# A two-stage spectral mix and a gated FFN on one core: unstrided PSUM columns and a hand-ordered opening

## Chip, cores, metric

One core of one Trainium2 chip runs the whole program. The metric is the device time of one execution in microseconds (us), as a median over runs. Engines are named as in the profile: PE is TensorE's matmuls, PEld its weight loads, DVE is VectorE, ACT is ScalarE, POOL is GpSimd, SP is the engine whose queue issues most DMAs; "SPq" is its queue.

## The reference

```python
X = np.fft.fft(x, axis=1)            # x: 8 batches x 3008 positions x 256 channels, fp32
X = np.fft.fft(X, axis=2).real       # keep the real part
x = X.reshape(24064, 256)
g, val = x @ w_gate, x @ w_val       # 256 -> 1536 each
out = (0.5 * g * (1 + erf(g / sqrt(2))) * val) @ w_out      # exact GELU, 1536 -> 256
```

## The kernel before

The transforms are done as matmuls with bf16 tables (G, CS, TPI) that the kernel computes itself with sines at its start. 3008 = 94 x 32 = 64 x 47, so one batch passes through these stages, each a small "pack" of matmuls into one PSUM tile followed by an evacuation:

- stage one, 16 packs: x (94 rows) against G, 96 columns a matmul, into A;
- second stage (CH), 12 packs: A against CS, 256 columns a matmul, into Z;
- E and O packs, 3 and 6: Z against TPI, 64 columns (E) or 2 x 64 columns (O), for 24 values k2, into EO. EO holds the even and odd halves of the tokens, in 23 x 64 + 33 columns.

The FFN then works on EO in three chunks of 512, 512 and 481 columns. Its first layer makes a result from E and O together, hands it to GELU and the product, and then adds a third matmul (weights M) on top of the same PSUM to get the mirrored tokens. The second layer sums 12 matmuls of 256 columns into the output. While batch b is in the FFN, the packs of batch b+1 are put between its matmuls as filler, so PE always has something to do.

The columns of neighbouring k2 are interleaved, so that a pair of them can be stored with one DMA whose rows are 2 KB:

```python
# cols: (offset in PSUM, k2, step, width) -- two k2 share 128 columns, alternating
if i + 1 < len(gr) and width(gr[i]) == width(gr[i + 1]):
    col += [(o, gr[i], 2, K1), (o + 1, gr[i + 1], 2, K1)]
...
def e_pack(gi):
    ps = ps_dft()
    for off, k2, step, n in cols[gi]:
        nc.tensor.matmul(_sub(ps, [[step, n]], off), Z[:, k2, 0:128], TPI[:, 0:n], ...)
    nc.scalar.activation(EO[E columns], ps[:, :n], AF.Copy)          # ScalarE evacuates E
def o_pack(gi, half):
    ps = ps_dft()
    for off, k2, step, n in part:
        nc.tensor.matmul(_sub(ps, [[256, 2], [step, n]], off - base), Z[:, k2, 128:256], TPI..., ...)
    nc.vector.tensor_copy(EO[O columns], ps[:, 256:256 + n])         # VectorE evacuates O
```

The opening. The first half of batch 0's x comes plain (fp32, SP's queue) and is cast by VectorE; the second half comes through GpSimd's queue, which casts on the way:

```python
load_x_plain([(0, 4), (4, 4), (8, 8)])            # SP: j 0..15, fp32
load_x(0, [(NJS, 8), (NJS + 8, 8)])               # GpSimd: j 16..31, cast by the DMA
...
gen_g(0, 8); cast_x(0, 4); gen_g(8, 24); cast_x(4, 4); cast_x(8, 8)
...                                               # w_gate, w_val by SP, w_out by GpSimd
for w in head[:NS1]: w()                          # stage one of batch 0
gen_cs(); gen_t()
for w in head[NS1:NHEAD]: w()                     # five CH packs, E and O of the first chunk
for nm in ("g", "v"): fold_w(nm, 0)()             # weights W: fold by an fp32 matmul, 512 columns
...
for b in range(B):
    if b + 1 < B:
        x_tiles.append(x_tile()); load_x(b + 1, [(0, 16), (16, 16)])   # GpSimd, casting
```

## Time and profile before

| | before |
|---|---|
| device time, median of 3 | 773.95 us (773.54 to 774.24) |
| span of the profiled run | 771.8 us |
| first first-layer matmul | 31.18 us |
| time from one batch's first first-layer matmul to the next, batches 2 to 6 | 91.5 us |

The page's busy table, and its chain of work that ended last:

```profile
PE 745.8 (97%) x5324; PEld 491.1 (64%) x5324; DVE 488.4 (63%) x829; ACT 442.1 (57%) x829; POOL 18.1 (2%) x39
...
PE 93%; ACT 2%; DMA 1%; DVE 1%; issue 1%; SPq 0%; ACTq 0%; DVEq 0%
```

PE is busy for 97% of the span and is 93% of the chain. So two things are worth working on: PE's own occupancy, and an earlier begin of the steady stage.

The groups by shape of the E (L376) and O (L389) matmuls. Columns: line, engine, operation, tiles, shape and count, then busy us and mean ns of one:

```profile
L350 PE MATMUL ps_dft<-CS,A_sb 128*128 128x256 bf16 x384 | 60.5, 280 | 0.3 <-ACT A_sb L332 0.3
...
L389 PE MATMUL ps_dft<-TPI,Z_sb 128*128 128x128 bf16 x184 | 26.7, 302 | 0.2 <-ACT EO_sb L379 0.2
...
L376 PE MATMUL ps_dft<-TPI,Z_sb 128*128 128x64 bf16 x184 | 16.9, 241 | 0.3 <-DVE Z_sb L360 0.3
```

The mean of an O matmul of 128 columns (302 ns) is longer than that of a contiguous CH matmul of 256 columns (280 ns). The records of neighbouring matmuls overlap (O matmuls start 109 ns apart, with records of 302 ns in the mean), so the better reading is from start to start.

The chain of waits through the opening, followed back from 34 us (start us, length us, what):

```profile
3.35 11.28 DMA wg_hi<-in_moe_w_gate_dram
...
14.76 2.05 PE ps_g L300 x2
...
17.45 1.71 PE ps_v L300 x2
...
24.30 4.80 PE ps_dft L350 x20
```

Two fp32 folds (PE ps_g and ps_v, L300) stand between stage-one packs (in the program's text they follow the CH packs; the trace shows the order that ran), and the five CH packs take 4.80 us: 20 matmuls, most of them 213 ns apart where the steady stage has 109. The clock records of this trace have TensorE at half rate there: half rate from 22.31 to 29.14 us, then full rate. Below, a stage is called cold when its CH matmuls stand 213 ns apart, warm when they stand 109 ns apart. The steady stage begins here:

```profile
31.18 0.42 PE L449 MATMUL ps_g<-EO_sb,WgE 128*128 128x512 bf16 x1
```

### The profile page before, as it was taken

The numbers are of one execution on the slowest core, as the hardware profiler recorded it, in microseconds if no ns is written. First come the engines' busy times: TensorE is split into PE (matmuls) and PEld (weight loads), VectorE is DVE, ScalarE is ACT, GpSimd is POOL, SyncE is SP. The second block draws the span as 40 slices with busy tenths as digits, with TensorE's granted clock in tenths as the row PEclk, the third lists the DMA queues.
The fourth block names the chain that finished last, engine by engine and source line by source line (L and its number), as shares of the span: only waits on it lengthen the run. The fifth ranks groups of instructions, "written<-read, shape, count | busy, mean of one in ns | idle before, by whom it ended". The sixth has DMA issues, their size and how long they took to land.

```text
span 771.8 us, 13825 instructions
## 1 busy us (share of the span) xinstructions
PE 745.8 (97%) x5324; PEld 491.1 (64%) x5324; DVE 488.4 (63%) x829; ACT 442.1 (57%) x829; POOL 18.1 (2%) x39
## 2 busy tenths in 40 slices
PE   3899999999999999999999999999999999999996
PEld 1555676666666666666666666666666666666565
DVE  6588666665666665766666666666566666655550
ACT  5656555555655555555655555555555555655552
POOL 6000000000000000000000000000000000000000
PEclk9899999999999999999999999999999999999999
DMA  9900501050101510114101320101010111011111
GB/s 237 237 12 24 112 28 42 28 118 28 43 28 39 112 38 28 42 38 108 41 30 42 78 69 28 42 28 40 28 42 29 39 36 34 28 42 38 42 42 65
DMA packets 32756, 42.54 MB, mean 55 GB/s; under 512 B 3770, under 2 KB 29370, under 8 KB 31282
## 3 DMA queue, kind: packets, MB, share of 16 engines
q1 hardware_dynamic: 29332, 29.34, 11.3%
q0 software_dynamic: 3360, 12.34, 8.4%
q8 instruction: 41, 0.67, 0.4%
q14 instruction: 23, 0.19, 0.1%
HBM read 29.36 MB, written 24.64 MB: 70 GB/s over the span
## 4 chain that ended last, share of the span: by engine, by line
PE 93%; ACT 2%; DMA 1%; DVE 1%; issue 1%; SPq 0%; ACTq 0%; DVEq 0%
PE ps_o L485 32%; PE ps_v L449 9%; PE ps_g L449 8%; PE ps_g L465 8%; PE ps_v L465 8%; PE ps_v L450 8%; PE ps_g L450 8%; PE ps_dft L350 5%; PE ps_dft L321 3%; PE ps_dft L389 3%; DMA wg_hi<-in_moe_w_gate_dram 1%; PE ps_dft L376 1%; ACT gelu_sb L469 1%; ACT gelu_sb L452 1%; DVE h_sb L453 1%
## 5 line engine op out<-in xcount | busy, mean ns | idle before, releaser
L453 DVE TENSOR_TENSOR h_sb<-gelu_sb,ps_v 128x512 bf16<-128x512 bf16 (+1 forms) x288 | 195.1, 678 | 203.7 <-ACT gelu_sb L452 138.3
L485 PE MATMUL ps_o<-Wo_sb,h_sb 128*128 128x256 bf16 (+1 forms) x2304 | 298.4, 273 | 0.0
L485 PEld LDWEIGHTS <-h_sb 128*128 128x128 bf16 (+1 forms) x2304 | 227.7, 100 | 74.4 <-issue 2.7
L452 ACT ACTIVATE gelu_sb<-ps_g 128x512 bf16<-128x512 f32 (+1 forms) x288 | 169.4, 588 | 161.8 <-PE ps_g L450 160.4
L471 DVE TENSOR_TENSOR h_sb<-gelu_sb,ps_v 128x512 bf16<-128x512 bf16 (+1 forms) x288 | 193.5, 672 | 45.0 <-ACT gelu_sb L469 42.6
L469 ACT ACTIVATE gelu_sb<-ps_g 128x512 bf16<-128x512 f32 (+1 forms) x288 | 169.2, 588 | 46.9 <-PE ps_g L465 44.9
L465 PE MATMUL ps_g<-EO_sb,WgM 128*128 128x512 bf16 (+1 forms) x288 | 110.0, 382 | 1.2 <-ACT gelu_sb L452 0.7
L449 PE MATMUL ps_g<-EO_sb,WgE 128*128 128x512 bf16 (+1 forms) x288 | 107.9, 375 | 1.3
L465 PE MATMUL ps_v<-EO_sb,WvM 128*128 128x512 bf16 (+1 forms) x288 | 108.2, 376 | 0.6
L449 PE MATMUL ps_v<-EO_sb,WvE 128*128 128x512 bf16 (+1 forms) x288 | 107.8, 374 | 0.8
L450 PE MATMUL ps_g<-EO_sb,WgO 128*128 128x512 bf16 (+1 forms) x288 | 108.1, 375 | 0.0
L450 PE MATMUL ps_v<-EO_sb,WvO 128*128 128x512 bf16 (+1 forms) x288 | 108.0, 375 | 0.0
L494 ACT ACTIVATE out_sb<-ps_o 128x512 f32<-128x512 f32 x96 | 57.3, 597 | 85.0 <-PE ps_o L485 85.0
L321 PEld LDWEIGHTS <-x_sb 94*128 94x128 bf16 x512 | 36.5, 100 | 44.4 <-issue 11.4
L350 PE MATMUL ps_dft<-CS,A_sb 128*128 128x256 bf16 x384 | 60.5, 280 | 0.3 <-ACT A_sb L332 0.3
L321 PE MATMUL ps_dft<-G,x_sb 94*128 94x96 bf16 x512 | 45.1, 210 | 13.8 <-ACT G L230 10.1
L350 PEld LDWEIGHTS <-A_sb 128*128 128x128 bf16 x384 | 37.8, 100 | 26.1 <-DVE A_sb L334 2.0
L360 DVE CAST Z_sb<-ps_dft 128x512 bf16<-128x512 f32 x69 | 47.2, 685 | 6.1 <-PE ps_dft L350 6.1
L334 DVE CAST A_sb<-ps_dft 128x384 bf16<-128x384 f32 x90 | 49.5, 552 | 1.8 <-PE ps_dft L321 1.5
L450 PEld LDWEIGHTS <-WvO 128*128 128x128 bf16 x288 | 28.0, 97 | 32.1 <-issue 11.1
L449 PEld LDWEIGHTS <-WvE 128*128 128x128 bf16 x288 | 28.2, 98 | 25.8 <-issue 1.1
L450 PEld LDWEIGHTS <-WgO 128*128 128x128 bf16 x288 | 28.1, 98 | 17.7 <-issue 8.4
(72 smaller groups left out, 318.1 us busy)
## 6 DMA issues: line engine op xcount, KB each, us to landing
out_dram<-out_sb SPq DMA_DIRECT2D x176, 128.0 KB, 2.0
x_sb<-in_x_dram POOLq DMA_DIRECT2D x14, 752.0 KB, 10.2
out_dram<-out_sb SPq DMA_DIRECT2D x16, 64.0 KB, 2.0
wg_hi<-in_moe_w_gate_dram SPq DMA_DIRECT2D x3, 256.0 KB, 9.1
wv_hi<-in_moe_w_val_dram SPq DMA_DIRECT2D x3, 256.0 KB
wg_lo<-in_moe_w_gate_dram SPq DMA_DIRECT2D x3, 256.0 KB, 8.5
wv_lo<-in_moe_w_val_dram SPq DMA_DIRECT2D x3, 256.0 KB
Wo_sb<-in_moe_w_out_dram POOLq DMA_DIRECT2D x2, 384.0 KB, 12.9
```

The lines of the kernel that those rows point to most:

```text
L321: nc.tensor.matmul(ps[:, jj * 96 : (jj + 1) * 96], xt[:, j0 + jj, cc * 128 : (cc + 1) * 128], G[:, j0 + jj, :], start=True, stop=True,)
L334: nc.vector.tensor_copy(dst, src)
L350: nc.tensor.matmul(ps[:, d * C : (d + 1) * C], A[:, cc, k2 + d, :], CS[:, cc, :], start=(cc == 0), stop=(cc == 1),)
L449: nc.tensor.matmul(ps[:, :n], W[nm, "E"][:, fs], EO[:, 0, c0 : c0 + n], start=True, stop=False)
L450: nc.tensor.matmul(ps[:, :n], W[nm, "O"][:, fs], EO[:, 1, c0 : c0 + n], start=False, stop=True)
L452: nc.scalar.activation(gl[:, :n], pg[:, :n], AF.Gelu)
L453: nc.vector.tensor_tensor(st["h"][:, fc, 0, :n], gl[:, :n], pv[:, :n], op=ALU.mult)
L465: nc.tensor.matmul(ps[:, :n], W[nm, "M"][:, fs], EO[:, 1, c0 : c0 + n], start=False, stop=True, skip_group_check=True)
L469: nc.scalar.activation(gl[:, :n], pg[:, :n], AF.Gelu)
L471: nc.vector.tensor_tensor(_sub(st["h"], [[-1, n]], (fc * 2 + 1) * TOK + n - 1), gl[:, :n], pv[:, :n], op=ALU.mult)
L485: nc.tensor.matmul(pso[:m, sign, :], st["h"][:, fc, sign, h0 : h0 + m], Wo_sb[:, fc, :], start=(fc == 0), stop=(fc == NFC - 1),)
L494: nc.scalar.activation(osb[:m], pso[:m], AF.Copy)
```

## The change

Its intent is to have PE write PSUM columns side by side, and to end the opening earlier. The whole of the first x is loaded plain by 96 rows (two of them only pad the count) and cast on VectorE and ScalarE; every engine's order in the opening is written by hand; the tables are computed with fewer, longer, contiguous calls; stage one and the five CH packs rotate over eight PSUM buffers instead of two; the first fold is 128 columns and the second 384. The stores double in number, since two k2 are no longer neighbours.

```diff
-            if i + 1 < len(gr) and width(gr[i]) == width(gr[i + 1]):
-                col += [(o, gr[i], 2, K1), (o + 1, gr[i + 1], 2, K1)]
-                ...
+        for k2 in gr:
+            col.append((o, k2, width(k2)))
+            o += width(k2)
@@ E pack, O pack
-                        _sub(ps, [[step, n]], off), ...
+                        ps[:, off : off + n], ...
-                        _sub(ps, [[256, 2], [step, n]], off - base), ...
+                        _sub(ps, [[256, 2], [1, n]], off - base), ...
@@ store: one DMA for each k2
-                ap=[[N2 * C, hi - lo], [1, n2 * C]],
+                ap=[[N2 * C, hi - lo], [1, C]],
@@ first x
-    xs = work_pool.tile([NP, NJS, C], ...)            # half of x, 94 rows in pieces of 80 and 14
+    xs = [work_pool.tile([96, NJ // 2, C], ...) for _ in range(2)]    # all of x
@@ PSUM of the opening
+    def ps_any(b):        # batch 0, first 24 packs: rotate over the tags dft, g, v, o
@@ opening
+    with tc.manual_schedule():
+        load_x_plain([(0, 4), (4, 4), (8, 8), (16, 8), (24, 8)])
+        load_w(); gen_consts()
+        g_phase(0, 8); g_sin(0, 8); cast_x(0, 4); g_phase(8, 24); s1_run(0)
+        cast_x(4, 4); cs_phase(); g_sin(8, 24); s1_run(4); cast_x(8, 8)
+        t_phase(); cs_sin(); t_sin()          # t_sin also loads GELU's table
+        ...                                   # keep, keep2
+        s1_run(8); s1_run(12)
+        cast_x(16, 4); cast_x(20, 4, True); s1_run(16)        # True: on ScalarE
+        cast_x(24, 4); cast_x(28, 4, True); s1_run(20); s1_run(24); s1_run(28)
+        for w in head[NS1:NHEAD]: w()
+        for nm in ("g", "v"): fold_w(nm, 0)()
+        ...
+        load_wo()
... (the table code itself, the column constants and the slots of the folds are cut)
```

Nothing in the diff touches the load of batch 1's x, but nothing holds it back either: GpSimd's queue used to be busy with half of batch 0's x and with w_out, and is now free.

## The prediction

> **What bounds the kernel now.** TensorE: the busy table has PE at 97% of a 771.8 us span, DVE 63%, ACT 57%, and the chain that ended last is 93% PE. From about 31 us (first first-layer matmul, L449, at 31.18 in the timeline) to 765 us the PE runs nearly back to back; in the windows 45-740 us it is busy 98-100%. So there are two places to win: shorter PE occupancy in the steady stage, and an earlier end of the opening.
>
> **PSUM columns unstrided (the larger part).** The E matmuls (L376, 64 columns) and O matmuls (L389, 2x64 columns) write PSUM at step 2. Read start to start in the trace, a 128-column O matmul holds the PE for 109 ns, just like the contiguous 256-column second-stage matmul L350 (109 ns), and a 64-column E matmul for 56 ns; the contiguous 33-column E and 66-column O ones take 30 ns. So strided writing runs at half speed. [...] Unstrided I estimate 56 and 29 ns: 53 + 27 = 80 ns per k2. 23 k2 x 7 batches x 80 ns = 12.9 us in the steady stage, and about 1.2 us for what batch 0 does after the opening. Those packs are filler between first-layer matmuls on a saturated PE, so nearly all of it counts; I deduct 1.5 us for slots that will then wait for GELU or an evacuation. The output stores double in number (each half as large, same 1 KB packets), off the chain.
>
> **Opening.** Now: DVE idles until 4.66 us, because the x cast stands first in its queue; the cosine table then needs ACT calls of 0.7-0.8 us for 192 elements and 1.55 us for 576 (strided bf16 writes), so the first matmul starts at 10.07; x pieces land at 4.6, 9.5, 14.2 us; two fp32 folds (2.05 and 1.91 us) sit between stage-one packs; stage one ends at 24.3; the second stage then runs at a clock of 0.59 (windows 25-30). After: tables first and half as many, contiguous ACT calls, first matmul near 5.5 us; stage one uses eight PSUM buffers, folds come later and the first is 128 columns wide, GELU's table load (1.28 us at 32.91) is early. But the order of instructions shows batch 1's x load (casting queue) right after the constants, near 3-4 us, without a wait: it shares the DMA engines with x, so I expect the last x piece at 17-20 us, stage one ending near 20-21, and a cold second stage again. First L1 matmul near 27 us: gain 4 us. The 384-column folds may give about 1 us back in the first slots.
>
> **Sum.** 773.95 - 12.9 - 1.2 + 1.5 - 4 + 1 = 758 us. Range 751 to 766. Chances: faster by over 2% 0.5, within 2% 0.48, slower 0.02.
>
> **What would show it.** O matmuls 56 ns apart and E near 30 (mean durations 302 to about 222, 241 to about 195 ns); steady windows shorter by 1.8 us per batch; first L1 matmul at 25-29 us; stage-one evacuations unchanged at 552 (DVE) and 492 ns (ACT).
>
> **What would make it wrong.** Stage-one evacuations now read PSUM one element at a time (step 48 between neighbours): if that is slower, DVE fills and PE waits (stage-one slots already hold most PE stalls). Weight loads, not columns, may bound E matmuls. The x load contention may eat the opening's gain, or prove mild and double it; Wo is now loaded last and could stall the second layer.

The sum: its 80 ns for each k2 is the estimate from the distances that stand before it, and the sum is 758 us (758.35 unrounded).

## More of the kernel before

The timeline of before around the first E and O packs in batch 1 (start us, length us, engine and line; only PE, DVE and ACT are copied):

```profile
177.25 0.61 PE L376 MATMUL ps_dft<-TPI,Z_sb 128*128 128x64 bf16 x8
...
177.66 0.41 PE L465 MATMUL ps_g<-EO_sb,WgM 128*128 128x512 bf16 x1
...
177.89 0.60 ACT L379 ACTIVATE EO_sb<-ps_dft 128x512 bf16<-128x512 f32 x1 [0.23 <-PE ps_dft L376]
177.91 0.38 PE L465 MATMUL ps_v<-EO_sb,WvM 128*128 128x512 bf16 x1
...
178.12 0.60 PE L389 MATMUL ps_dft<-TPI,Z_sb 128*128 128x128 bf16 x4
178.39 0.59 ACT L469 ACTIVATE gelu_sb<-ps_g 128x512 bf16<-128x512 f32 x1
...
178.52 0.42 PE L465 MATMUL ps_g<-EO_sb,WgM 128*128 128x512 bf16 x1
...
178.78 0.38 PE L465 MATMUL ps_v<-EO_sb,WvM 128*128 128x512 bf16 x1
...
179.03 0.38 PE L449 MATMUL ps_g<-EO_sb,WgE 128*128 128x512 bf16 x1
```

Eight E matmuls hold PE from 177.25 to 177.66: 0.41 us. Four O matmuls hold it from 178.12 to 178.52: 0.40 us, 109 ns each after the first. The 512-column matmul behind each pack then holds PE for longer than its usual 0.216 us: 0.25 us (177.66 to 177.91) and 0.26 us (178.52 to 178.78).

## The result, and the profile after

| | before | after |
|---|---|---|
| device time, median | 773.75 us (773.54 to 774.24) | 765.73 us (765.58 to 766.20) |
| ratio after : before | | 0.9897 [0.9879, 0.9914] |
| span of the profiled run | 771.8 us | 763.8 us |
| first first-layer matmul (weights WgE) | 31.18 us | 32.04 us |
| from there to the end | 740.6 us | 731.8 us |
| batch to batch, batches 2 to 6 | 91.5 us | 90.3 us |

The gain is 8 us, half of what was forecast. It lies 0.3 us inside the slow end of the range, and that is partly luck: the range was wide enough to take in an opening that lost time instead of gaining 4 us. A ratio is the mean time of one kernel's fast runs over that of the other's of the same rounds, so it is not quite the ratio of the medians quoted; brackets hold its 95% interval.

The busy table and the chain of after:

```profile
PE 733.6 (96%) x5328; PEld 477.1 (62%) x5328; DVE 490.1 (64%) x834; ACT 442.6 (58%) x828; POOL 12.4 (2%) x30
...
PE 91%; ACT 3%; DMA 3%; DVE 2%; issue 1%; SPq 0%; ACTq 0%
```

PE has lost 12.2 us of busy time and its share of the chain has gone down, while ACT, DMA and DVE have gained shares. That is the first sign that part of what PE gave up has come back as waiting.

The same groups by shape after:

```profile
L385 PE MATMUL ps_dft<-TPI,Z_sb 128*128 128x128 bf16 x184 | 17.3, 219 | 0.5 <-ACT EO_sb L375 0.5
...
L372 PE MATMUL ps_dft<-TPI,Z_sb 128*128 128x64 bf16 x184 | 12.1, 193 | 0.2
```

302 ns became 219 and 241 became 193, as forecast (about 222 and 195). The timeline at the same place of batch 1:

```profile
176.69 0.40 PE L372 MATMUL ps_dft<-TPI,Z_sb 128*128 128x64 bf16 x8
...
176.92 0.38 PE L457 MATMUL ps_g<-EO_sb,WgM 128*128 128x512 bf16 x1
...
177.12 0.60 ACT L375 ACTIVATE EO_sb<-ps_dft 128x512 bf16<-128x512 f32 x1
177.14 0.38 PE L457 MATMUL ps_v<-EO_sb,WvM 128*128 128x512 bf16 x1
...
177.14 0.69 DVE L445 TENSOR_TENSOR h_sb<-gelu_sb,ps_v 128x512 bf16<-128x512 bf16 x1 [1.33 <-ACT gelu_sb L444]
177.35 0.39 PE L385 MATMUL ps_dft<-TPI,Z_sb 128*128 128x128 bf16 x4
...
177.58 0.38 PE L457 MATMUL ps_g<-EO_sb,WgM 128*128 128x512 bf16 x1
...
177.61 0.59 ACT L461 ACTIVATE gelu_sb<-ps_g 128x512 bf16<-128x512 f32 x1
...
177.88 0.38 PE L457 MATMUL ps_v<-EO_sb,WvM 128*128 128x512 bf16 x1
...
178.26 0.38 PE L441 MATMUL ps_g<-EO_sb,WgE 128*128 128x512 bf16 x1
```

The E pack holds PE for 0.23 us (176.69 to 176.92) and the O pack for 0.23 us (177.35 to 177.58), each about half of before, and the matmul behind the E pack is back at 0.22 us. But the next two matmuls wait. The one at 177.88 adds to ps_v, which the product on DVE (177.14 to 177.83) is still reading; the one at 178.26 takes the ps_g that GELU on ACT (177.61 to 178.20) is still reading, and that GELU stood behind E's evacuation (L375, from 177.12). From the start of the E pack to the matmul at 178.26 it is 1.57 us; the same piece of before (177.25 to 179.03) took 1.78 us. Two packs and their tails that became 0.42 us cheaper (0.41 + 0.03 to 0.23, and 0.40 + 0.04 to 0.23) gained 0.21 us here.

The chain through the opening of after:

```profile
2.58 19.72 DMA x_plain<-in_x_dram
...
22.33 0.70 DVE x_sb L225
...
23.93 0.88 ACT A_sb L329 x2
...
24.86 1.20 PE ps_g L347 x4
```

The first first-layer matmul of after:

```profile
32.04 0.39 PE L441 MATMUL ps_g<-EO_sb,WgE 128*128 128x512 bf16 x1
```

One DMA of x is on the chain for 19.72 us, until 22.31 us. What SP's queue waits for in the first 40 us shows the same (total us, times, longest us), before and then after:

```profile
SPq L285 <- DMA x_plain<-in_x_dram: 6.4, 3, 3.8
```

```profile
SPq L268 <- DMA x_plain<-in_x_dram: 16.1, 4, 6.2
```

The last piece of x landed at 22.3 us (before: 13.9). From 8 to 22 us the packets of batch 1's x, in GpSimd's queue, are in the trace beside those of batch 0's. SP's queue moves 524 to 574 KB in 2 us while it is alone and 213 to 311 KB while both are busy, about half.

### The profile page after: what moved, and what is told of

Read it like the earlier page. It is cut to its first block, busy times and chain, and to the rows that moved or that the text cites. A ratio compares the mean times of both kernels' runs of the same rounds, so it can differ in the third digit from the quotient of the medians.

```text
span 763.8 us, 14086 instructions
## 1 busy us (share of the span) xinstructions
PE 733.6 (96%) x5328; PEld 477.1 (62%) x5328; DVE 490.1 (64%) x834; ACT 442.6 (58%) x828; POOL 12.4 (2%) x30
## 4 chain that ended last, share of the span: by engine, by line
PE 91%; ACT 3%; DMA 3%; DVE 2%; issue 1%; SPq 0%; ACTq 0%
PE ps_o L477 32%; PE ps_v L441 9%; PE ps_g L441 9%; PE ps_g L457 8%; PE ps_v L457 8%; PE ps_v L442 8%; PE ps_g L442 8%; PE ps_dft L347 4%; DMA x_plain<-in_x_dram 3%; PE ps_dft L318 2%; ACT gelu_sb L461 1%; PE ps_dft L385 1%; DVE h_sb L445 1%; ACT gelu_sb L444 1%; PE ps_dft L372 1%
## 5 line engine op out<-in xcount | busy, mean ns | idle before, releaser
L457 PE MATMUL ps_g<-EO_sb,WgM 128*128 128x512 bf16 (+1 forms) x288 | 108.3, 376 | 1.0 <-ACT gelu_sb L444 0.7
L347 PE MATMUL ps_dft<-CS,A_sb 128*128 128x256 bf16 x360 | 56.0, 274 | 0.0
L331 DVE CAST A_sb<-ps_dft 128x384 bf16<-128x384 f32 x84 | 46.1, 551 | 0.5 <-PE ps_dft L318 0.2
L357 DVE CAST Z_sb<-ps_dft 128x512 bf16<-128x512 f32 x65 | 44.4, 684 | 0.3 <-PE ps_dft L347 0.3
L318 PE MATMUL ps_dft<-G,x_sb 94*128 94x96 bf16 x464 | 41.8, 208 | 0.0
```

The costliest lines, as they stand in the source:

```text
L318: nc.tensor.matmul(ps[:, jj * 96 : (jj + 1) * 96], xt[:, j0 + jj, cc * 128 : (cc + 1) * 128], G[:, j0 + jj, :], start=True, stop=True,)
L331: nc.vector.tensor_copy(dst, src)
L347: nc.tensor.matmul(ps[:, d * C : (d + 1) * C], A[:, cc, k2 + d, :], CS[:, cc, :], start=(cc == 0), stop=(cc == 1),)
L457: nc.tensor.matmul(ps[:, :n], W[nm, "M"][:, fs], EO[:, 1, c0 : c0 + n], start=False, stop=True, skip_group_check=True)
```

## The experiments

Theory of the steady stage: the gain comes from PSUM columns alone, and part of it turns into waits for ACT and DVE. Rival: the rest of the change (eight PSUM buffers, early tables) carries a part. Theory of the opening: batch 1's x takes the DMA engines from batch 0's x. Rivals: the vector work of the tables, ScalarE's, or PE's clock bounds it. All twelve kernels gave correct results. Some of the texts count the strided writes as costing 1.49 us a batch because the first strided matmul of a pack seemed to be free; the reading of the tails, further down, came after them.

### e1: batch 1's x behind the weights

```diff
         load_wo()
+        x_tiles.append(x_tile())
+        load_x(1, [(0, 16), (16, 16)])
...
-            x_tiles.append(x_tile())
-            load_x(b + 1, [(0, 16), (16, 16)])
+            if b: (the same two lines)
```

> The changed kernel with one thing moved: batch 1's x load (casting queue) is issued after W_out instead of right after the constants. Theory 1, contention: the opening is bound by the arrival of x, which shares the DMA engines with that load (pieces 4 and 5 land at 15.8 and 22.3 us in the changed kernel). Then the last x piece lands near 15 us (10-us pieces at the 270 GB/s that the queue moved before the second load began), stage one ends near 17.5, the first first-layer matmul comes near 25 us instead of 32.04, and the time is 758 to 760 us. Rival 1: the opening is bound by its own chain (tables, casts, cold clock, folds); then x lands earlier but the first first-layer matmul moves by less than 1.5 us and the time stays at 764 or more.

Measured: 762.32 us, ratio 0.9847 [0.9832, 0.9862]; 3.4 us better than after. The last x landed at 15.45 us instead of 22.3, and SP's wait fell from 16.1 us to this:

```profile
SPq L268 <- DMA x_plain<-in_x_dram: 9.4, 4, 2.8
```

So the contention is shown. But the last stage-one evacuation came at 21.88 us only (25.19 in after), where 17.5 was expected, and the time missed its 758 to 760. The chain of this kernel through its opening tells why:

```profile
12.97 0.46 DVE col_n L245
...
14.87 0.30 DVE rd L196
15.19 0.31 ACT TPI L257
15.52 1.28 ACT L259
17.02 1.11 ACT A_sb L329 x3
```

The vector operations of the last table, its sine and GELU's table load (ACT L259, 1.28 us) stand ahead of stage one's evacuations and casts. The hand-written order put them there as if x were late in any case.

### e2: before, with the PSUM columns and stores of after alone

The edit is the first, second and third part of the diff above, on the kernel before.

> The kernel before with only the PSUM columns unstrided (and the stores that follow from it); its opening is untouched. Theory: all of the measured gain comes from here. In the traces the packs hold the PE 1.49 us less per batch, 0.2 us of it comes back as waits for GELU, so 1.28 us per batch: time 764 to 766 us, no slower than the changed kernel and perhaps 0.5 to 1 us faster, with the first first-layer matmul at 30.5 to 31 us. Rival: the new opening gives part of the gain; then this run is slower than the changed kernel, 768 us or more.

Measured: 764.11 us, ratio 0.9871 [0.9856, 0.9886]: 10.0 us better than before and 1.6 us better than after. The columns bring the whole gain.

### e3: after, with strided columns and paired stores again

The same edit reversed, on after.

> The changed kernel with the old strided PSUM columns and paired stores: the new opening alone. Theory: the new opening gains nothing, the first first-layer matmul is at 32 to 32.6 us and the time is 774 to 775 us, at or just above the kernel before. Rival: the opening gains 2 us or more and the time is 772 or less.

Measured: 775.67 us, ratio 1.0016 [0.9999, 1.0033]. The new opening by itself gains nothing; by its median it costs 1.5 us, which is also the difference of e2 and after. The two parts add up.

### e4: columns interleaved by runs of two

Two k2 share 128 columns, but two neighbouring columns of one, then two of the other: a non-contiguous pattern whose runs are 8 bytes. The stores are mapped to match.

```diff
-                        ps[:, off : off + n], ...
+                        _sub(ps, [[4, n // 2], [1, 2]], off), ...
```

> The changed kernel with the columns of two k2 interleaved again, but in runs of two: a matmul writes two neighbouring columns, skips two, and so on; stores are remapped, the result stays right. [...] pairs run like unstrided columns: 56 ns from one O matmul to the next and 29 ns between E matmuls, time within 0.5 us of the changed kernel (765.7). If any gap in the output pattern costs, O matmuls stay at 109 ns and the time is near 774.

Measured: 766.43 us, ratio 0.9901 [0.9886, 0.9916], as after within the interval (by its median 0.7 us slower, where 0.5 was allowed for). Its groups by shape:

```profile
L392 PE MATMUL ps_dft<-TPI,Z_sb 128*128 128x128 bf16 x184 | 17.3, 219 | 0.5 <-ACT EO_sb L382 0.5
...
L379 PE MATMUL ps_dft<-TPI,Z_sb 128*128 128x64 bf16 x184 | 12.1, 193 | 0.1
```

To the nanosecond these are the means of after (219 and 193 ns), where single columns at step 2 had 302 and 241 in before. So this pattern of pairs, though non-contiguous, adds nothing to the means; the pattern of single columns held PE for twice the time (109 ns instead of 55 to 56 for 128 columns, start to start in before and after). The runs show what each pattern takes, not why.

### e5: e1, with the last table and GELU's table load behind stage one

```diff
-        t_phase()
         cs_sin()
-        t_sin()
...
         s1_run(28)
+        t_phase()
+        t_sin()
```

> The first experiment's kernel (batch 1's x load after W_out) with the tables of the last transform step (nine VectorE instructions, one sine call, GELU's table load) moved from the middle of stage one to behind it. In the first experiment x no longer bounded stage one (last piece at 15.5 us, last evacuation done near 21.9): theory, the program's own order does, because these instructions stand in front of stage-one evacuations in VectorE's and ScalarE's queues (VectorE 12.8 to 15.3 us, ScalarE 15.2 to 17.0). Then stage one ends 2.5 to 4 us earlier, near 18 to 19 us, and the time is 758.5 to 760.5. Rival: the casts and evacuations themselves fill both engines, and stage one ends less than 1 us earlier; time 761.5 or more.

Measured: 759.63 us, ratio 0.9813 [0.9797, 0.983]: 2.7 us better than e1. The last stage-one evacuation came at 18.73 us (21.88 in e1), as expected. Together e1 and e5 gain 6.1 us on after: this is what the opening cost by two mistakes of order.

### e6: e5, with idle matmuls of 94 rows to release PE's clock

```diff
+                if b == 0 and cc == 0 and j0 >= 8:
+                    for _ in range(4):
+                        nc.tensor.matmul(ps[:, 0:384], xt[:, j0 - 8, 0:128], G[384 columns], ...)
```

> The previous kernel (tables later) plus idle-time matmuls: from the ninth row on, four 384-column matmuls on x rows that are already there, into the PSUM tile that the next stage-one pack overwrites. In all kernels so far the first 16 to 20 second-stage matmuls start 213 ns apart instead of 109. Theory: [...] keeping the PE busy before makes them 109 ns apart and gains 1.5 to 2.5 us against the previous kernel. Rival: something else than PE activity paces them (weights, PSUM, DMA traffic) and they stay near 213; the time is unchanged or up to 1 us worse, for the PE has more to do.

Measured: 765.36 us, ratio 0.9886 [0.9872, 0.9901]. This was a miss, 5.7 us slower than e5. PE worked without a pause from 13.4 us to the end of stage one, but the clock's records show full rate from 27.46 us only. The timeline of PE:

```profile
21.04 1.48 PE L319 MATMUL ps_o<-G,x_sb 94*128 94x384 bf16 x4
22.31 0.53 PE L323 MATMUL ps_o<-G,x_sb 94*128 94x96 bf16 x4
...
24.42 1.06 PE L352 MATMUL ps_v<-CS,A_sb 128*128 128x256 bf16 x4
...
26.98 0.84 PE L352 MATMUL ps_g<-CS,A_sb 128*128 128x256 bf16 x4
```

Four idle matmuls of 384 columns hold PE from 21.04 to 22.31, 0.32 us each: 0.83 ns a column, as in the cold CH matmuls (213 ns for 256 columns; 109 ns, 0.43 a column, in warm ones). The first four CH packs stay at 0.85 us or more (213 ns a matmul), and the idle work delayed stage one to 23.75 us. That a busy PE gets the full clock was the assumption, and this run does not show it.

### e7: after, with E's evacuation on VectorE for batches 1 to 7

```diff
-                nc.scalar.activation(EO[...], ps[:, :n], AF.Copy)
+                (nc.vector.tensor_copy if b else nc.scalar.activation)(...)
```

> The changed kernel with the evacuation of the E packs (0.6 us each) on VectorE instead of ScalarE for batches 1 to 7. In the changed kernel's trace new PE waits of 60 to 220 ns for GELU follow the E packs, 0.2 to 0.35 us per batch, which the kernel before did not have. Theory: the faster E packs reach the next first-layer matmul before ScalarE, held by the E evacuation, has done the GELU; then these waits go and the time falls by 1 to 2 us, to 763.7 to 764.7. Rival: the waits come from the PSUM buffers whoever evacuates; then VectorE's queue is the new place of the wait and the time stays within 0.5 us or rises.

Measured: 764.33 us, ratio 0.9874 [0.9857, 0.989]; 1.4 us better than after. Marked at the same matmuls, a batch is 0.375 us shorter than in after (mean over batches 1 to 7). The size is as the theory says. Its mechanism is not: from 140 to 580 us PE's waits for a product on DVE fell from 9.2 to 7.1 us, but those for GELU, which the freed ScalarE should have shortened, stayed (5.4 in after, 5.6 here). This trace lacks 61 of 5328 matmul records, whose gaps were left out of these sums.

### e8: e5, with x in 16 pieces of two rows

```diff
-        load_x_plain([(0, 4), (4, 4), (8, 8), (16, 8), (24, 8)])
+        load_x_plain([(j, 2) for j in range(0, NJ, 2)])
```

> The kernel with the tables later, with the first x loaded in 16 pieces of two rows (2 KB runs) instead of five of four or eight rows (4 and 8 KB). In the traces the same queue moves 2 KB packets of the gate weights at 387 GB/s and the 8 KB packets of x at about 260. Theory: the packet size is the cause; x is complete near 11 to 12 us instead of 15.2, the weights follow earlier, and the time falls up to 2 us if stage one can follow. Rival: the 96 rows are the cause (the weights fill 128 partitions), or the sync queue's issue (about 0.43 us a DMA) and its eight outstanding DMAs; then x still ends at 15 us or later and the time is the same or worse.

Measured: 758.34 us, ratio 0.9797 [0.9782, 0.9812]. The last x landed at 15.28 us, just as in e5, where 11 to 12 was expected, so that theory fell: from 2 to 14 us SP's queue moved 520 to 572 KB in 2 us (by the starts of the packets), against 469 to 561 in e5. By its median it is 1.3 us better than e5. The first four rows had landed at 4.0 us (4.6 in e5) and the clock rose at 21.45 us (23.67); which of these brought the gain was not tested. The limit of eight DMAs that the rival names can be read in after's timeline: SP issues its 12th and 13th DMA at 15.77 and 22.32 us, just as the fourth and fifth piece of x land (15.8 and 22.3), so eight are under way each time.

### e9: e8, with idle matmuls of 128 rows

Six fp32 matmuls of 256 columns, of two constant tiles, stand ahead of stage-one packs, the first three from 9.69 us on.

```diff
+                if b == 0 and cc == 0:
+                    for _ in range({8: 3, 16: 1, 20: 1, 24: 1}.get(j0, 0)):
+                        nc.tensor.matmul(ps[:, 0:256], exch, row_c, start=True, stop=True)
```

> The 2 KB kernel (batch 1's x late, tables later, x in 2 KB pieces; 758.3 us) plus six idle-time matmuls on all 128 rows (fp32, 256 columns, operands ready since the constants): three before the third stage-one group, one before each of the next three. The clock records show that no kernel with the new opening gets the full clock before 3 to 5 us into the second stage, and that the 94-row idle matmuls did not release it though they kept the PE busy from 13.4 us on; in the kernels with the old opening it was released at 18.9 us, behind the 128-row fp32 folds. Theory: 94-row matmuls do not count as activity enough, 128-row ones do; then the record of the full clock comes before 18.5 us, second-stage matmuls start 109 ns apart from the first on, and the time falls by 1 to 2 us to 756.5 to 757.5. Rival: [...] the clock is still released at 21 us or later and the time is 758.3 to 759.5 (the idle matmuls delay stage one).

Measured: 758.70 us, ratio 0.9801 [0.9787, 0.9816]: no gain on e8, where 1 to 2 us were expected. Yet the clock is at full rate from 13.40 us, 3.7 us after the first three idle matmuls began. The timeline, with ScalarE's table load:

```profile
19.11 0.60 PE L350 MATMUL ps_o<-CS,A_sb 128*128 128x256 bf16 x4
...
19.55 0.60 PE L350 MATMUL ps_dft<-CS,A_sb 128*128 128x256 bf16 x4
19.64 1.28 ACT L259 ACT_TABLE_LOAD   x1
...
21.05 0.57 ACT L358 ACTIVATE Z_sb<-ps_v 128x512 bf16<-128x512 f32 x1
```

CH packs now come 0.44 us apart (109 ns a matmul). But GELU's table load (ACT L259) begins at 19.64, and the pack that ended near 19.3 waits for its evacuation until 21.05. A cold second stage had hidden that load (e12 moves it and stays within 0.12 us of e10); a warm one runs into it.

What frees the clock is narrowed down by this, not settled. In e6 matmuls of 94 rows that kept PE busy without a pause from 13.4 us did not free it: full rate came at 27.46 us, 4.0 us after the 128-row CH matmuls began at 23.42. Here three of 128 rows (fp32, 256 columns), begun at 9.69 us, were followed by full rate at 13.40. In e11 the same three, begun at 9.84 us, and a fourth at 13.81 had it at 15.12 only. The two kinds of idle matmul differ in their type too (bf16 and fp32), but the 128-row matmuls after which it came in e6 were bf16. How many rows it takes was not measured.

### e10: e8, with e7's edit

> The 2 KB kernel with the E evacuation of batches 1 to 7 on VectorE: the two gains put together. The opening and the steady stage do not overlap, so if both are real they add: VectorE evacuation gave 1.4 us on the changed kernel (765.7 to 764.3), so 756.5 to 757.3 here. If that 1.4 us was partly the opening's scatter (its first first-layer matmul came 0.5 us later than in the changed kernel) the batches each get 0.2 to 0.3 us shorter and the sum is the same; if the gain was noise the time is 758 or more.

Measured: 757.23 us, ratio 0.9784 [0.9767, 0.98]: 1.1 us better than e8, so the edit adds as it did to after.

### e11 and e12: GELU's table load behind the five CH packs, with and without idle matmuls

Both have E on VectorE. e11 is e9 with the edit below, e12 is e10 with it.

```diff
+        t_cols()          # five small vector operations of the last table, ahead of s1_run(8)
...
         for i, w in enumerate(head[NS1:NHEAD]):
+            if i == 5:
+                nc.scalar.activation(dump, col_p[0:1, :], AF.Gelu)      # out of t_sin
             w()
```

> Question left by the kernel with 128-row idle matmuls (758.70 us, no gain over 758.34 although its clock was free from 13.4 us and its second stage began at 17.95): what held the time between 20 and 24 us? Theory: in its timeline the activation table for GELU loads on ScalarE from 19.64 to 20.92 us, exactly while the second stage's packs wait there for their evacuation (a pack done near 19.3 is evacuated from 21.05 on); with a cold second stage this load was hidden, with a warm one it is not. This kernel moves the load behind the five second-stage evacuations and the five small vector operations of the last table ahead of the last x pieces, and takes E's evacuation to VectorE for batches 1 to 7 as well. Theory: first WvE matmul near 24.5 us (25.45 there), 256-column second-stage matmuls still 109 ns apart, and 756 to 756.5 us (E on VectorE is worth 1.1 of it). Rival: idle matmuls themselves or something later bound it; then first WvE stays near 25.4 and the time near 757.3.

> The same move of the GELU table load and of the five small operations, without idle matmuls, on the kernel that took 757.23 us. Theory: with a cold second stage (213 ns at its start) little or nothing is gained, because the load was hidden: first WvE near 26 us, 756.8 to 757.4 us, so 0.5 to 1 us behind the warm one. Rival: if the load bound the cold one as well, it comes within 0.3 us of the warm one and the clock is worth nothing here.

Measured: e11 756.89 us, ratio 0.9781 [0.9767, 0.9794]; e12 757.35 us, ratio 0.9785 [0.9772, 0.9799]. e12 is as expected: with a cold second stage the move gains nothing (e10: 757.23). e11 missed its landmark: its first WvE matmul is at 25.33 us, not 24.5. Its timeline:

```profile
19.46 0.60 ACT L358 ACTIVATE Z_sb<-ps_v 128x512 bf16<-128x512 f32 x1 [0.32 <-PE ps_v L350]
...
20.95 1.28 ACT L549 ACT_TABLE_LOAD   x1
...
22.35 0.57 ACT L381 ACTIVATE EO_sb<-ps_dft 128x512 bf16<-128x512 f32 x1
...
22.97 0.38 PE L391 MATMUL ps_dft<-TPI,Z_sb 128*128 128x128 bf16 x4 [1.03 <-ACT EO_sb L381]
```

The CH packs are now evacuated at once (ps_v at 19.46 instead of 21.05), but the load from 20.95 on holds back E's evacuation until 22.35, and the last O pack (22.97) waits 1.03 us for that. The wait has moved to the next user of ScalarE. A free clock saves 1.3 us up to the first WvE matmul (25.33 against 26.64 in e12), of which the times show 0.5, and their ranges overlap (756.52 to 757.41 and 757.03 to 757.55). Whether a better place for the load would give the rest was not tried.

| kernel | us | ratio to before |
|---|---|---|
| after | 765.73 | 0.9897 |
| e3 after, strided again | 775.67 | 1.0016 |
| e2 before, unstrided | 764.11 | 0.9871 |
| e1 batch 1's x later | 762.32 | 0.9847 |
| e5 and last table later | 759.63 | 0.9813 |
| e8 and x in 16 pieces | 758.34 | 0.9797 |
| e10 and E on VectorE | 757.23 | 0.9784 |
| e11 and table load moved, clock freed | 756.89 | 0.9781 |

e10 beats before with few edits, by 16.4 us of before's 773.61 us in its own rounds.

## Why the prediction was right or wrong

**The bound and the strided writes: right.** PE was the bound (97% busy), and strided columns held it for twice the time: 109 and 56 ns start to start (O and E). O and E matmuls lost 83 and 48 ns in the mean, unstrided ones stand 56 and 29 ns apart, and stage one's evacuations kept their time (551 ns on DVE after, 552 before; 489 on ACT, 492 before), although they read PSUM in another order. The size is right too, though the way it comes about was not foreseen. The prediction counted 80 ns for each of 23 k2, 1.84 us a batch. Measured start to start, the packs of a batch hold PE 1.49 us less, because the first strided matmul of a pack holds it hardly longer than an unstrided one (65 to 69 ns against 55 to 57 for O, 28 to 30 for E in both). The missing part sits behind the packs: in before the successor of the matmul after a strided pack starts late, by 42 ns behind a four-matmul O pack and by 27 to 29 ns behind most E packs. Behind one E pack of a batch it is 57 ns, but there the successor starts 0.05 us after the end of the GELU that frees its ps_g (285.89 and 285.84 us in one batch), so a part of that is a wait. With it the tails are 0.31 us a batch, and in after they are gone. Together it is 1.80 us a batch at most. That the total came so near the forecast 1.84 is luck in part: one part was counted too high and another not at all.

**"I deduct 1.5 us for slots that will then wait for GELU or an evacuation": right in kind, too small.** The batch became 1.24 us shorter, not 1.80, so about 0.56 us a batch came back. Read start to start from 140 to 580 us (about five batches), PE's waits of over 40 ns, tails left out, grew from 11.6 to 14.7 us, which is 0.6 a batch: those for GELU from 3.2 to 5.4 us, those for DVE's product from 8.3 to 9.2. They stand before a matmul that needs a ps_v that the product still reads, or a ps_g that GELU still reads, as shown at 177.88 and 178.26. With strided packs PE had arrived later by just so much, and the wait was hidden in the slower matmul. e7 takes E's evacuation off ScalarE and gets 0.375 us a batch back. Over the whole kernel e2 gives the size of the term: the columns alone gained 10.0 us, where 12.9 and 1.2 less 1.5 make 12.6; the waits are therefore about 4 us (14.1 - 10.0, an estimate that takes the first two terms as right) instead of 1.5.

**"First L1 matmul near 27 us: gain 4 us": wrong; this is the step that failed.** It came at 32.04 us, 0.86 later than before, and the opening cost 1.5 us by e3's median (the interval of its ratio, 0.9999 to 1.0033, just takes in no change). The mechanism had been named: batch 1's x shares the DMA engines. It was mis-sized. The last piece landed at 22.3 us where 17 to 20 was expected, so stage one ended at 25.19 where 20 to 21 was expected; and behind it came the cold second stage (CH packs of 0.85 us or more, most of their matmuls 213 ns apart, full rate recorded from 28.79 us), which was foreseen. e1 shows the cause by removing it: x at 15.45 us and 3.4 us of time. e5 shows what the forecast did not name at all: even with x on time, the order written by hand places the last table and GELU's table load ahead of the work that x feeds, another 2.7 us. With both mended the gain on before is 14.5 us (774.16 to 759.63), near what the forecast of 16 us asked for.

**Smaller points.** First matmul near 5.5 us: right (5.37). It was worth nothing, since the chain ran through the last x and not the first. "384-column folds may give about 1 us back": not separated from the rest of the opening; of the 1.5 us, after's trace puts 0.86 ahead of the first first-layer matmul, so some 0.6 would lie behind it. The sine calls of before that wrote bf16 at a stride took 1.53 to 1.62 us for 576 elements a row; those of after, which write side by side, take 1.50 and 1.52 us for 1152. Twice as many stores: no effect seen; they land in 2.0 us as before, and from the start of the last output evacuation to the end it is 6.57 us (6.46 before). w_out loaded last: no stall of the second layer seen.

**Left open.** Why e7 shortened the waits for the product and not those for GELU; what brought e8's gain; and how much a fully clear warm second stage would bring.

## What to carry to other kernels

On a saturated engine, cost an occupancy from start to start, include the instruction behind it, and then ask who else must be ready by the earlier time: here a third of what PE saved was lost at once to a GELU and a product that had been just in time. This opening was bound first by its last input and not by its first matmul, so before working on the first matmul, look at which loads share the DMA engines with that input, a load that the diff does not touch included (3.4 us in e1). A hand-written order is only as good as the arrival times that it assumes: put what nobody needs yet (the last table, an activation's table load) behind the work that arriving data feeds (2.7 us in e5), and look again after each repair, since the wait moved here (e9, e11).
